# A gated linear-attention and bilinear-GLU kernel on one core: gate/up and q products in another seven-product form, more output rows in seven products, and an order that is computed in the builder

## The chip, the core and the metric

The kernel runs on one core of a Trainium2 chip. The core has a matrix engine (TensorE: PE, with its weight loads shown as PEld), a vector engine (VectorE: DVE), a scalar engine (ScalarE: ACT), a general engine (GpSimd: POOL) and SyncE (SP). In this kernel SP and POOL mostly issue DMAs; those that add to what is already in the destination are issued by POOL. Each engine works through its own list of instructions in the order of the program, and semaphores make it wait for the others.

The metric is the device time of one execution in microseconds (us). Three runs of the kernel before took 590.53, 592.59 and 592.73 us; the median is 592.59.

## What is computed

```python
def _A_ref(x, wqkv, wo):                      # linear attention, 32 heads of 16
    qkv = ...                                 # x @ wqkv, split in q, k, v
    phi = lambda t: jnp.where(t > 0, t + 1, jnp.exp(t)) + 1e-6
    pq, pk = phi(q), phi(k)
    kv = jnp.einsum("bhsd,bhse->bhde", pk, v)
    z = jnp.einsum("bhsd->bhd", pk)
    num = jnp.einsum("bhqd,bhde->bhqe", pq, kv)
    den = jnp.einsum("bhqd,bhd->bhq", pq, z)[..., None] + 1e-6
    return (num / den, heads joined) @ wo

def _B_ref(x, w_gate, w_up, w_down):          # bilinear GLU
    h = (x @ w_gate) * (x @ w_up)
    return h @ w_down

g = _sigmoid((x * gate_w).sum(-1, keepdims=True))
out = g * a + (1 - g) * b
```

x is 2048 x 512 (tokens by features), the hidden width of the GLU is 1792, everything is float32.

## The kernel before, in words

**Numbers in two parts.** A float32 operand is split in a rounded high part (an ACT copy) and a low part (a DVE subtraction), and a product is three matmuls: high by high, high by low, low by high (`mm3`, line 79 for every matmul). So nearly all matmuls have the same shape, 128 x 128 by 128 x 512.

**Phase 1** (16 tiles of 128 tokens) makes k, its feature map and the sums that attention needs (tiles `pk`, `gt`). Beside it x is split for the first pair, and the weights of the first two units are got ready: a dictionary `todo` says after which token tile each step is issued.

**Phase 2** works on transposed data: the tokens in two pairs of blocks of 512 columns, and for each pair 16 *units*. A unit is one 128-wide slice of gate and up (14 of them, kind "f") or one pair of q slices (2 of them, kind "q"). Its 2 x 2 block product (two token blocks by two weights, each sum over two halves of the features) is done in seven products of six matmuls each in place of eight (`unit`, from line 523): sums of x blocks (`xa`, `xb`, `xc1`, `xc4`, `xc6`) and sums of weight blocks (`wr`, split to `wch`, `wcl`) go in, and the products gather in four PSUM banks Y, X, R and S.

**A unit's weights.** `w_load` gets three blocks of 128 x 256, `w_add` makes four more on ACT (two instructions of 512 columns) and adds to five blocks with one POOL DMA of 640 KB, `w_high` and `w_low` split all seven in three parts. There are two raw buffers (`wr`) and two of each split part, so the load for unit n+2 can begin when unit n's weights are split.

**Down projection.** A hidden slice and its rows of w_down (or an attention slice and rows of a product with wo) is one *row*; two rows are a *row pair*. A plain row pair is eight jobs of six matmuls (`down_jobs`, tile `pdn`), each job's result added on DVE to an accumulator `acc`. In the seven-product form (`seven`, banks `sa` and `sb`) a row pair is seven jobs of six matmuls, and several row pairs are chained in one *lot*, so that PSUM is emptied once in a lot; each job needs a split x block (ACT and DVE), and each step a split block of weights (`ws`, `wh`, `wl`), some of them sums made by POOL DMAs. Of the 18 row pairs, 12 are in the seven-product form (four in the first token pair, eight in the second).

**The order.** The units are written out by hand with ten named places in each (`PLACES`). The tables `FIRST` and `SECOND` say how many jobs go to PE between which products; other tables say at which place a step of attention, a load or a split is issued; `advance` lets the chains of the next jobs proceed by leads.

Of the kernel before, what the change touches and what calls it, by code (L numbers as in the profile page):

```python
# [31 lines left out]
LEAD_X = 4  # L32
LEAD_W = 17
GAP_L = 6
GAP_A = 14
HB = 8
FIRST_SEVEN = (((4, 5), (6, 7)), (('a', 0), (8, 9)))
FIRST_AT = (4, 8)
MINUS_AT = (1, 2, 3)
XAT = (11, 6, 4, 8, 11, 7, 11, 13, 13, 13, 10, 13)  # L40
WUNIT = (8, 5, 2)
FIRST = (
    (3, 1, 3, 0), (0, 3, 2, 1), (0, 0, 1, 1), (2, 0, 1, 0), (0, 1, 0, 2), (0, 0, 0, 1), (1, 2, 0, 2), (0, 3, 0, 0),
    (0, 0, 2, 2), (0, 2, 3, 1), (2, 1, 1, 1), (3, 2, 0, 2), (2, 0, 1, 0), (3, 3, 3, 3), (1, 2, 0, 0), (3, 0, 2, 3),
)
PLACES = "high low e m c d t s r end".split()
ATT = ((0, 8, 5, 4, 6, 4, 5, 3), (0, 5, 12, 5, 0, 9, 4, 13))
NS = 58
SECOND = (
    (2, 1, 1, 0), (0, 0, 1, 3), (2, 1, 0, 3), (1, 0, 0, 0), (0, 1, 0, 2), (0, 0, 1, 2), (2, 0, 0, 2), (0, 2, 0, 1),  # L50
    (0, 2, 1, 2), (2, 2, 2, 0), (0, 0, 2, 1), (0, 3, 3, 1), (0, 3, 1, 0), (2, 2, 0, 1), (3, 0, 2, 3), (3, 1, 0, 2),
)
STARTS = (0, 4, 4, 10)
MOST = (2, 2, 2, 2)
MOST_0 = (1, 1, 2, 2)
LEAD_X0 = 4
LEADS_0 = (15, 7, 12)
RELOAD = ((0, 1), (0, 2), (3, 4), (5, 6))
Q_AFTER = ((5, 9), (0, 3))

SLOT = {3: 0, 4: 1, 2: 2, 5: 3, 1: 4, 6: 5, 7: 6}
# [3 lines left out]
def gated_mix(ctx: ExitStack, tc, xt, xp, x, wqkv, wq, wq_add, wo, wgu, wgu_add, wdn, gate_w, out):  # L71
# [39 lines left out]
    def dma_add(dst, src):  # L111
# [17 lines left out]
    own = {i: [const.tile([P, 2, CH], F32R, name=f"xc{i}{v}") for v in "hl"] for i in (1, 4, 6)}  # L129
    xc = {2: [v[:, 0:2] for v in xa], 7: [v[:, 2:4] for v in xa],  # L130
          3: [v[:, 0:2] for v in xb], 5: [v[:, 2:4] for v in xb], **own}


    zeros = own[1][0][:, 0, 0:CH // 2].bitcast(mybir.dt.bfloat16)
# [9 lines left out]
    xsum = {i: dram.tile([P, 2, CH], F32, name=f"xsum{i}") for i in (1, 5, 6, 7)}  # L144
# [28 lines left out]
    def w_add(n):  # L173

        if n < len(order):
            _, kind, m = order[n]
# [12 lines left out]
    def w_low(n, part):  # L189
        if n < len(order):  # L190
# [5 lines left out]
    SUMS = {1: (A1, B2, 0), 3: (B1, B2, 1), 4: (A2, A1, 1), 6: (A1, B1, 0), 7: (A2, B2, 0), 2: (None, A1, 0),  # L196
            5: (None, B2, 0)}

    def x_load(tile_, pair, i, ks):
        dma(tile_, xp[pair, SUMS[i][1]][:, ks])  # L200

    def x_add(tile_, pair, i, ks):
        one, _, sub = SUMS[i]
        if sub:
            act(tile_, tile_, scale=-1.0)
        if one is not None:
            dma_add(tile_, xp[pair, one][:, ks])
# [4 lines left out]
    with tc.tile_pool(name="p1", bufs=2, reuse_waits="tile") as p1:  # L212
# [127 lines left out]
        def cb_load(i):  # L340
            cbs[i] = p1.tile([P, 2, CH], F32, tag="cbs", name="cbs", bufs=3)
            x_load(cbs[i], 0, i, slice(0, 2))

        for t, i in zip((6, 7, 9, 10, 12), (4, 1, 6, 7, 3)):
            plan(t, lambda i=i: cb_load(i))
            plan(t + 2, lambda i=i: x_add(cbs[i], 0, i, slice(0, 2)))
            plan(t + 5, lambda i=i: split(*xc[i], cbs.pop(i)))
        for n, t in ((0, 8), (1, 11)):
            plan(t, lambda n=n: w_load(n))
            plan(t + 2, lambda n=n: w_add(n))  # L350
        plan(14, lambda: w_high(0))
        for part in range(3):
            plan(14 + part // 2, lambda part=part: w_low(0, part))
        plan(16, lambda: w_load(2))
# [36 lines left out]
    p2 = ctx.enter_context(tc.tile_pool(name="p2", bufs=1, reuse_waits="tile"))  # L391
    live = []
    spare, kept = [], {}

    class Buf:

        def __init__(self, name, rounded=False):
            self.home = rounded and bool(spare)
            one = spare.pop(0) if self.home else p2.tile([P, CH], F32R if rounded else F32, tag="s", name=name, bufs=NS)
            self.f = one.bitcast(F32) if rounded else one  # L400
            self.r = one
            if not self.home:
                live.append(self)
                assert len(live) <= NS, clock[0]

    def put(*some):
        for one in some:
            if one.home:
                spare.append(one.r)
            else:  # L410
                live.remove(one)

    def two(name):
        return [Buf(name + v, True) for v in "hl"]

    def split_buf(name, src, copy="act"):

        hi, lo = two(name)
        split(hi.r, lo.r, src, copy)
        return hi, lo  # L420


    at = {}

    def later(n, place, fn):
        at.setdefault((n, place), []).append(fn)

    def do(n, place):
        for fn in at.pop((n, place), []):
            fn()  # L430
        clock[0] += 1
# [13 lines left out]
    def always():  # L445
        return True
# [800 lines left out]
```

## Time and profile before

| what | value |
|---|---|
| median of three runs | 592.59 us |
| the profiled execution, first to last instruction | 591.5 us |
| TensorE clock granted, mean | 0.999 |
| PE busy | 583.7 us (99%) |
| DVE busy | 491.3 us (83%) |
| ACT busy | 364.9 us (62%) |
| POOL busy | 100.3 us (17%) |
| moved by DMA | 106.19 MB |

Busy times are those of the instructions themselves. Matmuls overlap in the pipeline (one is shown as some 390 ns, while the next begins 227 ns later), so PE time is best read from the starts of matmuls: how many begin in a stretch, and where a stretch has fewer. The view by windows gives such counts, the view of waits names who released an engine that stood idle, and the chain that ended last shows the work in order of time.

### The profile page before, as it was taken

What the parts mean: (1) busy time and instruction counts of PE and PEld (TensorE: products, weight loads), DVE (VectorE), ACT (ScalarE), POOL (GpSimd) and SP (SyncE); (2) the same over time, 40 slices, a digit from 0 to 9 for tenths busy, and PEclk for the clock granted to TensorE, in tenths of its full rate; (3) what the DMA queues carried; (4) which work ended last, traced back from release to release, by engine and by line L of the source; (5) the groups of instructions that cost most, each with busy time, mean ns of one, the idle gap of its engine ahead of it and who ended that gap; (6) DMA issues with size and microseconds to landing.
All of it is one profiled execution on the core that took longest, in us unless ns stands there. A gap on an engine that the chain in (4) does not pass through costs nothing.

```text
span 591.5 us, 7915 instructions
## 1 busy us (share of the span) xinstructions
PE 583.7 (99%) x2610; PEld 478.0 (81%) x2610; DVE 491.3 (83%) x798; ACT 364.9 (62%) x649; POOL 100.3 (17%) x123
## 2 busy tenths in 40 slices
PE   9999999999999999999999999999999999999997
PEld 6888888888888868788888788888888888888886
DVE  6877895775567889999869967998798999799987
ACT  3856774677647475688456747458956846646520
POOL 0011100000151124111020042305010322301000
PEclk9999999999999999999999999999999999999999
DMA  9476946868898879556798699779875676834003
GB/s 296 168 201 129 284 106 197 213 194 225 252 225 205 204 211 208 146 120 161 213 239 248 211 221 224 226 155 244 215 168 133 176 148 148 186 71 63 0 2 142
DMA packets 68249, 106.19 MB, mean 180 GB/s; under 512 B 8864, under 2 KB 40352, under 8 KB 68192
## 3 DMA queue, kind: packets, MB, share of 16 engines
q1 hardware_dynamic: 51872, 68.98, 35.5%
q0 software_dynamic: 16048, 36.18, 34.9%
q10 hardware_dynamic: 288, 0.52, 0.3%
q8 instruction: 20, 0.33, 0.2%
q14 instruction: 21, 0.17, 0.1%
HBM read 90.70 MB, written 15.61 MB: 180 GB/s over the span
## 4 chain that ended last, share of the span: by engine, by line
PE 90%; DVE 5%; issue 2%; DMA 2%; ACT 1%; POOL 0%; DVEq 0%; POOLq 0%; ACTq 0%
PE bY L79 13%; PE bX L79 13%; PE bR L79 13%; PE sa L79 11%; PE pdn L79 9%; PE sb L79 8%; PE pk L79 8%; PE gt L79 7%; PE bS L79 7%; DMA wr<-in_wgu_add 2%; DVE wcl L88 1%; DVE acc L88 1%; PE warm L79 1%; PE pw L79 0%; DVE cross L88 0%
## 5 line engine op out<-in xcount | busy, mean ns | idle before, releaser
L88 DVE TENSOR_TENSOR wcl<-wr,wch 128x512 fp32r<-128x512 f32 (+1 forms) x96 | 73.2, 772 | 2.0 <-ACT wch L85 1.9
L85 ACT ACTIVATE wch<-wr 128x512 fp32r<-128x512 f32 (+1 forms) x96 | 60.3, 691 | 4.9 <-DMA wr<-in_wgu_add 4.6
L112 POOL DMA_DIRECT2D wr<-in_wgu_add x28 | 25.0, 892 | 207.7 <-ACT wr L85 153.4
L79 PE MATMUL bX<-xbh,wch 128*128 128x512 f32 x128 | 47.3, 390 | 0.0
L79 PE MATMUL bX<-xbl,wch 128*128 128x512 f32 x128 | 47.2, 389 | 0.0
L79 PE MATMUL bX<-xbh,wcl 128*128 128x512 f32 x112 | 43.6, 389 | 0.0
L85 ACT ACTIVATE cross<-bY 128x512 f32<-128x512 f32 x32 | 19.0, 594 | 33.4 <-PE bY L79 33.3
L88 DVE TENSOR_TENSOR bR<-bX,m 128x512 f32<-128x512 f32 x32 | 22.2, 695 | 20.5 <-PE bX L79 19.6
L85 ACT ACTIVATE m<-bY 128x512 f32<-128x512 f32 x32 | 19.0, 593 | 31.7 <-PE bY L79 31.7
L112 POOL DMA_DIRECT2D ws<-dminus x27 | 31.1, 1341 | 35.7 <-DVE wl L88 24.7
L85 ACT ACTIVATE wr<-wr 128x512 f32<-128x512 f32 x64 | 36.4, 618 | 0.3 <-DMA wr<-in_wgu 0.3
L85 ACT ACTIVATE xh<-cross 128x512 fp32r<-128x512 f32 x38 | 23.5, 626 | 20.7 <-DVE cross L88 19.7
L88 DVE TENSOR_TENSOR t<-bR,cross 128x512 f32<-128x512 f32 x32 | 22.0, 687 | 15.0 <-PE bR L79 6.9
L88 DVE TENSOR_TENSOR acc<-pdn,acc 128x512 f32<-128x512 f32 (+1 forms) x39 | 25.4, 671 | 8.1 <-PE pdn L79 7.9
L85 ACT ACTIVATE cross<-bX 128x512 f32<-128x512 f32 x32 | 19.0, 593 | 21.3 <-DVE bS L88 21.2
L79 PEld LDWEIGHTS bX<-xbh,wch 128*128 128x128 f32 x128 | 24.0, 188 | 5.3 <-ACT cross L85 0.3
L79 PEld LDWEIGHTS bX<-xbl,wch 128*128 128x128 f32 x128 | 24.0, 188 | 5.0
L88 DVE TENSOR_TENSOR xl<-cross,xh 128x512 fp32r<-128x512 f32 x38 | 25.9, 684 | 2.4 <-ACT xh L85 2.2
L79 PE MATMUL bS<-xah,wch 128*128 128x512 f32 x64 | 25.1, 392 | 0.7 <-DVE bS L88 0.7
L112 POOL DMA_DIRECT2D ws<-in_wdn x18 | 24.1, 1721 | 9.1 <-DMA ws<-in_wdn 9.1
L79 PE MATMUL pdn<-hl,dh 128*128 128x512 f32 (+1 forms) x65 | 25.2, 388 | 0.0
L79 PE MATMUL pdn<-hh,dl 128*128 128x512 f32 (+1 forms) x65 | 25.1, 386 | 0.0
(310 smaller groups left out, 1823.6 us busy)
## 6 DMA issues: line engine op xcount, KB each, us to landing
wr<-in_wgu_add POOLq DMA_DIRECT2D x28, 640.0 KB, 6.9
wr<-in_wgu SPq DMA_DIRECT2D x28, 384.0 KB
ws<-in_wdn SPq DMA_DIRECT2D x45, 128.0 KB
xraw<-in_x SPq DMA_DIRECT2D x16, 256.0 KB
terms<-zq SPq DMA_DIRECT2D x16, 256.0 KB
zt<-terms SPq DMA_DIRECT2D x16, 256.0 KB
rb<-den SPq DMA_DIRECT2D x16, 256.0 KB
ws<-dminus POOLq DMA_DIRECT2D x27, 128.0 KB, 4.8
```

Source lines behind the costliest of these rows:

```text
L79: tc.keep_in_program_order(nc.tensor.matmul(*args, **kw))
L85: pin(nc.scalar.activation(dst, src, func, **kw))
L88: pin(nc.vector.tensor_tensor(dst, a, b, op=op))
L112: tc.keep_in_program_order(nc.gpsimd.dma_start(dst, src, accum_op=ALU.add))
```

## The change

Nothing changes in what is computed or in the matmul work of phase 1. Four things are different.

1. **Units: seven products in a form with chained sums.** The products run in the order 1, 5, 6, 2, 7, 3, 4 through banks Y, X, R, Y, R, S, R. Product 1 is copied from Y to R by ACT, product 6 is added to it there, then product 7 and product 4 go on in the same bank; product 5 is copied out once by ACT (`m5`) and added twice by DVE. DVE makes two sums in a unit where it made three; ACT makes three copies in both.
2. **A unit's weights: one chain of sums.** Each new block is the sum before it with one block more, so four blocks are made instead of four copies and five additions in one DMA: ACT copies 256 columns, POOL adds 128 KB, ACT copies 256, POOL adds 128 KB, ACT copies 512, POOL adds 256 KB, each waiting for the one ahead. Blocks 0 to 2 need no sum and are split first. The sums of x are chained in the same way.
3. **Down projection.** 16 of 18 row pairs are in the seven-product form. Lots have one to three row pairs (table `LINE`); the first row pair of the first token pair and the last of the second are plain.
4. **The order.** Phase 2 is written down first as a list of operations with a cost and the buffers that they read and write (`mix`). A model of the engines and DMA rings is then played in the builder (`run`): PE takes from two lines, units and jobs, so that the count of jobs follows the table `SHARE`; each other engine takes the ready operation with the earliest due time. The order in which the model started them is the order of the program. The tables of places are gone.

```diff
-    def w_add(n):
-            act(raws[n][:, 3:5], raws[n][:, 0:1].to_broadcast([P, 2, 2 * P]))
-            act(raws[n][:, 5:7], raws[n][:, 0:2], scale=-1.0)
-            dma_add(raws[n][:, 2:7], (wgu_add if kind == "f" else wq_add)[m])
-    PARTS = ((0, 2), (2, 4), (4, 7))
+                act(raw[:, 3:4], raw[:, 2:3])
+                dma_add(raw[:, 3:4], more[:, 0:1], 0.72)
+                act(raw[:, 4:5], raw[:, 3:4], scale=-1.0)
+                dma_add(raw[:, 4:5], more[:, 1:2], 0.72)
+                act(raw[:, 5:7], raw[:, 4:5].to_broadcast([P, 2, 2 * P]))
+                dma_add(raw[:, 5:7], more[:, 2:4], 1.41)
+    PARTS = ((0, 3), (3, 5), (5, 7))
...
+            product(1, "Y", True)
+            act(bk["R"], bk["Y"])
+            product(5, "X", True)
+            act(m5.f, bk["X"])
+            product(6, "R")
+            tt(bk["S"], bk["R"], m5.f, ALU.add)
+            product(2, "Y")
+            act(cross[0].f, bk["Y"], scale=-1.0 if turned[0] else 1.0)
+            product(7, "R")
...
+                tt(cross[1].f, bk["R"], m5.f, ALU.add)
+            product(3, "S")
+                tt(cross[1].f, bk["S"], cross[1].f, ALU.mult)
+            product(4, "R")
+            tt(cross[0].f, bk["R"], cross[0].f, ALU.mult)
...
-FIRST_SEVEN = (((4, 5), (6, 7)), (('a', 0), (8, 9)))
+LINE = (
+    (0, ((0, 1),)),
+    (0, ((2, 3), (4, 5), (6, 7))),
+    (0, (('a', 0), (8, 9), (10, 11))),
+    (0, ((12, 13), ('a', 1))),
+    (1, ((0, 1), (2, 3))),
+    (1, (('a', 0), (4, 5), (6, 7))),
+    (1, (('a', 1), (8, 9), (10, 11))),
+    (1, ((12, 13),)),
+)
...
+                if engine == "PE":
+                    some = [heads[s][at[s]] for s in "uj" if at[s] < len(heads[s])]
+                    if len(some) == 2 and at["j"] < share(at["u"]):
+                        some.reverse()
+                    for op in some:
+                        if open_[op] and may(op, t):
+                            return take(op, t)
+                    return
+                for op in sorted(ready[engine], key=lambda op: (late[op], op.id)):
+                    if may(op, t):
+                        return take(op, t)
```

Three places show what this does to the lists of the engines. The first is ACT in unit 3 of the first token pair (units count from 0), before: the weights of unit 4 are split in one go (`wch_1475` from the raw blocks `wr_1251`), and the raw blocks of unit 5 (`wr_1385`) get both of their instructions behind them, ahead of unit 3's last bank copy (`cross1_1451<-bX_1396`).

```order
L85 ACTIVATE cross0_1450<-bY_1395 128x512
L85 ACTIVATE half_1303<-half_1303 128x512
L85 ACTIVATE pws_1469<-pw_1465 128x512
L85 ACTIVATE minus_1472<-pws_1469 128x256
L85 ACTIVATE wch_1475<-wr_1251 128x512 x2
L85 ACTIVATE wch_1475<-wr_1251 128x768
L85 ACTIVATE wr_1385<-wr_1385 128x512 x2
L85 ACTIVATE minus_1492<-wdr_1198 128x256
L85 ACTIVATE cross1_1451<-bX_1396 128x512
```

Now the raw blocks of unit 4 are `wr_1252` and their split is `wch_1403`. In unit 2, two of the three instructions on them and the first two parts of the split stand among the bank copies `m5_1328` and `cross0_1365`, with the first ones for unit 5 (`wr_1341`):

```order
L504 ACTIVATE m5_1328<-bX_1308 128x512
L504 ACTIVATE minus_1338<-wdr_1156 128x256
L504 ACTIVATE wr_1252<-wr_1252 128x256
L504 ACTIVATE minus_1343<-pws_1303 128x256
L504 ACTIVATE minus_1346<-wdr_1166 128x256
L504 ACTIVATE cross0_1365<-bY_1291 128x512
L504 ACTIVATE wr_1341<-wr_1341 128x256
L504 ACTIVATE wr_1252<-wr_1252 128x512
L504 ACTIVATE pws_1393<-pw_1322 128x512
L504 ACTIVATE wch_1403<-wr_1252 128x768
L504 ACTIVATE wch_1403<-wr_1252 128x512
L504 ACTIVATE wr_1341<-wr_1341 128x256
```

The last part of unit 4's split stands behind the first bank copy of unit 3 (`bR_1417`):

```order
L504 ACTIVATE bR_1417<-bY_1396 128x512
L504 ACTIVATE wch_1403<-wr_1252 128x512
L504 ACTIVATE minus_1429<-pws_1393 128x256
L504 ACTIVATE m5_1441<-bX_1422 128x512
L504 ACTIVATE wr_1341<-wr_1341 128x512
```

What moved: where one instruction in a unit's turn needed the landing of a POOL DMA (the first of the split), three do now (the second and third `wr<-wr`, and the last of the split), each with bank copies behind it; a unit's split still ends within the unit ahead of it.

The second place is POOL in the same units, before: one addition for each unit, with an x block of the second pair (`cb`) among them.

```order
L112 DMA wr_1251<-in_wgu_add 128x1280
L112 DMA wr_1385<-in_wgu_add 128x1280
L112 DMA wr_1534<-in_wq_add 128x1280
L112 DMA cb_1636<-in_xp 128x512
L112 DMA wr_1671<-in_wgu_add 128x1280
```

Now, three for each unit, and nothing else among them:

```order
L526 DMA wr_1252<-in_wgu_add 128x256 x2
L526 DMA wr_1341<-in_wgu_add 128x256
L526 DMA wr_1252<-in_wgu_add 128x512
L526 DMA wr_1341<-in_wgu_add 128x256
L526 DMA wr_1341<-in_wgu_add 128x512
L526 DMA wr_1433<-in_wq_add 128x256 x2
L526 DMA wr_1433<-in_wq_add 128x512
L526 DMA wr_1520<-in_wgu_add 128x256 x2
L526 DMA wr_1520<-in_wgu_add 128x512
```

What moved: each unit's one addition is three, and the x block stands behind these units now.

The third place is DVE in one unit, before: three sums through the banks (`bR`, `t`, `bS`), with three parts of the next unit's split (`wcl`) among them, and two gate products (`cross1`, `cross0`).

```order
L88 TENSOR_TENSOR bR_1397<-bX_1396,m2_1399 128x512
L88 TENSOR_TENSOR hl_1373<-cross0_1286,hh_1372 128x512
L88 TENSOR_TENSOR dl_1417<-wdr_1198,dh_1416 128x512
L88 TENSOR_TENSOR t_1489<-bR_1397,cross0_1450 128x512
L88 TENSOR_TENSOR wcl_1476<-wr_1251,wch_1475 128x512
L88 TENSOR_TENSOR bS_1398<-t_1489,bX_1396 128x512
L88 TENSOR_TENSOR wcl_1476<-wr_1251,wch_1475 128x512
L88 TENSOR_TENSOR wcl_1476<-wr_1251,wch_1475 128x768
L88 TENSOR_TENSOR cross1_1451<-bR_1397,cross1_1451 128x512
L88 TENSOR_TENSOR cross0_1450<-bS_1398,cross0_1450 128x512
```

Now two sums (`bS` and `cross1`, both with `m5`), the two gate products, and the split in a piece of its own:

```order
L511 TENSOR_TENSOR wcl_1407<-wr_1252,wch_1403 128x768
L511 TENSOR_TENSOR wcl_1407<-wr_1252,wch_1403 128x512 x2
L511 TENSOR_TENSOR bS_1450<-bR_1417,m5_1441 128x512
L511 TENSOR_TENSOR cross1_1476<-bR_1417,m5_1441 128x512
L511 TENSOR_TENSOR cross1_1476<-bS_1450,cross1_1476 128x512
L511 TENSOR_TENSOR cross0_1461<-bR_1417,cross0_1461 128x512
```

What moved: a sum is gone, and the next unit's split (`wcl_1407`) stands in one piece ahead of the sums, not between them.

Counted over the whole lists, PE has 2564 rows where it had 2588 (matmuls, the eight weight loads of the warm-up and two branches; 192 fewer write `pdn`, 168 more write `sa` and `sb`, and the units' number is the same), DVE 767 where it had 784, ACT 730 where it had 653, and the additions to `wr` that POOL issues are 96 where there were 32.

More of the change, by code (lines that the diff above doesn't have):

```diff
@@ L1 @@
+import heapq
 from contextlib import ExitStack
@@ L406, in put @@
[L406 to L431, printed above, removed]
-        most = MOST if n >= units else MOST_0
-        advance(dve=most[0], act=most[1])
@@ L1143, in plain @@
-    def plain(n):
-        return order[n][1] == "f" and (order[n][0], order[n][2]) not in row_of
-    ffn = [n for n in range(len(order)) if plain(n)]
-    def d_load(i):
-        if i < len(ffn):
-            n = ffn[i]
-            wdr[n] = Buf("wdr")
-            dma(wdr[n].f, wdn[order[n][2]])
-    d_load(0)
-    wp_load()
-    g_evac()
-    d_load(1)
-    rows = []
-    for some, place in SEVEN:
-        later(units + place, "end", lambda some=some: jobs.extend(
-            seven(1, [fps[1, key] for key in some], some == SEVEN[-1][0])))
@@ L1198 @@
+        for pair, some in LINE:
+            if len(some) == 1:
+                plain(pair, some[0])
+            else:
+                seven(pair, some)
+        plan(todo_ops, units)
+    mix()
 def kernel(A_x, A_wqkv, A_wo, B_x, B_w_gate, B_w_up, B_w_down, gate_w):
```

1475 lines of the change are left out of this document (791 added, 684 removed).

## The prediction

> **What bounds the kernel now.** I read the page's first part and the chain that ended last, then the windows, then the waits of PE, then the chain in order of time.
>
> ```profile
> span 591.5 us, 7915 instructions
> PE 583.7 (99%) x2610; PEld 478.0 (81%) x2610; DVE 491.3 (83%) x798; ACT 364.9 (62%) x649; POOL 100.3 (17%) x123
> ...
> PE 90%; DVE 5%; issue 2%; DMA 2%; ACT 1%; POOL 0%; DVEq 0%; POOLq 0%; ACTq 0%
> ```
>
> PE is the bound: it is busy nearly all the time, and nine tenths of the chain is matmul work. A busy PE need not be at its peak, so I count how many matmuls (x) begin in equal stretches. The columns are the stretch, its length, the busy times of PE, PEld, DVE, ACT and POOL, the granted clock, the DMA share and GB/s.
>
> ```profile
> 200.00:250.00 50.00, 48.69 (x211) 38.71 (x209) 44.95 (x72) 28.78 (x52) 12.37 (x14) 1.00 0.81 193
> 250.00:300.00 50.00, 49.30 (x215) 39.97 (x215) 46.58 (x77) 36.76 (x67) 5.22 (x6) 1.00 0.69 165
> 300.00:350.00 50.00, 49.31 (x217) 40.14 (x216) 40.75 (x62) 31.05 (x52) 7.13 (x9) 1.00 0.85 240
> 350.00:400.00 50.00, 50.00 (x222) 41.28 (x221) 44.65 (x72) 27.35 (x49) 15.05 (x20) 1.00 0.82 199
> 400.00:450.00 50.00, 50.00 (x222) 41.39 (x221) 44.24 (x73) 40.06 (x74) 11.45 (x13) 1.00 0.80 195
> ...
> 550.00:570.00 20.00, 20.00 (x90) 16.57 (x89) 19.65 (x32) 9.44 (x17) 0.00 (x0) 1.00 0.00 1
> ```
>
> A stretch of 50 us without a stall holds 222 matmuls, and the clock is full throughout. Three stretches hold 211, 215 and 217, so 11 + 7 + 5 = 23 matmuls are missing. The last row says something else: with DVE busy for 19.65 of 20 us PE still lost nothing. A full DVE is not in itself a stall.
>
> ```profile
> PE sb L79 <- ACT xh L85: 1.1, 1, 1.1
> PE sa L79 <- ACT xh L85: 0.7, 1, 0.7
> PE bS L79 <- DVE bS L88: 0.7, 1, 0.7
> PE sb L79 <- DVE xl L88: 0.2, 1, 0.2
> ...
> 1.26 3.61 PE warm L79 x8
> ...
> 348.23 5.44 PE pdn L79 x24
> ...
> 576.80 11.02 PE pdn L79 x54
> ```
>
> The waits say who was late: three times a split x block for a job of a seven-product lot (`sa`, `sb`), once a DVE sum within a unit (`bS`). The last rows are pieces of the chain (start, length). They give the pitch, 5.44 / 24 = 0.227 us a matmul, so the 23 missing ones are **5.2 us** of stalls. They also give the ends: 1.3 us before the first matmul, and 591.5 - 576.80 - 11.02 = 3.7 us behind the last piece. Both ends do the same work after the change.
>
> **The change, part by part.** *Matmuls removed.* Four more row pairs go from eight jobs to seven, six matmuls each: 24 fewer, as the lists say (2588 to 2564). The row of 24 matmuls above prices them without any conversion: **-5.4 us**. They stand on the bound, so all of it is gained unless PE waits more. Units keep their 42 matmuls, phase 1 its own.
>
> *Stalls removed.* The order that caused the 5.2 us no longer exists. I take all of them out and put the new order's in by three terms. None of the three can be below nothing, since the old stalls are already out.
>
> ```profile
> L85 ACT ACTIVATE cross<-bY 128x512 f32<-128x512 f32 x32 | 19.0, 594 | 33.4 <-PE bY L79 33.3
> L85 ACT ACTIVATE wch<-wr 128x768 fp32r<-128x768 f32 x32 | 26.6, 833 | 0.0
> L85 ACT ACTIVATE wch<-wr 128x512 fp32r<-128x512 f32 x64 | 36.8, 620 | 4.9 <-DMA wr<-in_wgu_add 4.6 <-DMA wr<-in_wq_add 0.3
> L88 DVE TENSOR_TENSOR bR<-bX,m 128x512 f32<-128x512 f32 x32 | 22.2, 695 | 20.5 <-PE bX L79 19.6 <-ACT m L85 0.6
> L88 DVE TENSOR_TENSOR wcl<-wr,wch 128x768 fp32r<-128x768 f32 x32 | 30.4, 949 | 0.0
> ```
>
> *(i) Hand-overs within a unit.* Product 6 adds to what ACT copied from Y to R, and only product 5 lies between: 6 x 0.227 = 1.36 us of cover. The copy is like `cross<-bY`, 0.594 us. If ACT has just begun a wide split (0.833), the two take 1.43 us, so a bad case costs 0.1 us and some hand-over, 0.3 at most as I estimate it. The sum into S (0.695, behind a `wcl` of 0.949) is alike. Bounds: 0 to 32 x 0.3 = 10 us. The nearest row is the old form's own hand-over of this kind, which cost (`bS`) a wait of 0.7 us in 32 units. I take 1.
>
> *(ii) The chain of weight sums.*
>
> ```profile
> wr<-in_wgu_add POOLq DMA_DIRECT2D x28, 640.0 KB, 6.9
> ...
> ws<-dminus POOLq DMA_DIRECT2D x27, 128.0 KB, 4.8
> ...
> cb<-in_xp POOLq DMA_DIRECT2D x10, 256.0 KB, 6.4
> ...
> ws<-in_wdn POOLq DMA_DIRECT2D x18, 128.0 KB, 6.6
> ...
> 60.52 0.43 SPq L109 DMA_DIRECT2D wr<-in_wgu  x1
> ...
> 67.25 1.15 ACT L85 ACTIVATE wr<-wr 128x512 f32<-128x512 f32 x2 [0.32 <-DMA wr<-in_wgu]
> ```
>
> The last number of a DMA row is its median time from issue to landing. One addition of 6.9 us becomes three, one behind the other: 4.8 + 4.8 + 6.4 = 16.0 us. The load took up to 67.25 - 60.52 = 6.7 us. With three ACT instructions (at most 0.62 each) and the last split (0.62 + 0.68) a raw buffer is held for some 6.7 + 1.9 + 16.0 + 1.3 = 25.9 us. There are two buffers, so PE keeps its pace where two units last longer. An early unit with one job beside it is 48 matmuls, 10.9 us, and two are 21.8 us: short by 4.1 us. But in those units POOL issues nothing else (the lists in the section on the change), while the medians come from crowded stretches.
>
> ```profile
> DMA to landing us min/median/max: 5.8/6.9/9.8
> DMA to landing us min/median/max: 2.9/6.0/11.8
> DMA to landing us min/median/max: 3.8/6.4/11.2
> ```
>
> These are the answers for the tiles `wr`, `ws` and `cb`. At the minima the chain is 2.9 + 2.9 + 3.8 = 9.6 us and the buffer is held for 19.5 us, less than 21.8; later units have some four jobs each (112 and 16 plain ones for 32 units) and last 15 us. The lists also end a unit's split within the unit ahead, so a late chain has most of a unit to give before PE waits for weights. What can hurt at once is ACT itself: it stands in the wait for a landing with a bank copy behind it. Bounds: 0, and 4.1 / 2 x 8 early units = 16 us. I take 1.5, near the lower end, because of the empty queue and of that slack.
>
> The Trainium skill, page "DMA: Bandwidth & Descriptors", sections "Anatomy of one DMA — SWDGE (gpsimd) path" and "Rules for kernel authors", speaks against this edit: each DMA has a fixed cost of about 2.0 us beside bytes / 436e3, and many small transfers should be made one. By its figures, one of 640 KB is an estimated 3.5 us and the three are 7.2 us, so the chain would grow by 3.7 us and still fit, and this term would be 0. The trace's 640 KB took 5.8 us at best, so the rows disagree with the size and I keep to them; that splitting costs is common to both.
>
> *(iii) Jobs of the seven-product form.* Most of the old stalls were theirs: 2.0 of the 2.7 us of waits above, so by that share 3.9 of the 5.2 us, in 12 x 7 = 84 jobs. There are 16 x 7 = 112 now. Bounds: 0, and at the old rate 3.9 x 112 / 84 = 5.2 us.
>
> ```profile
> L88 DVE TENSOR_TENSOR acc<-pdn,acc 128x512 f32<-128x512 f32 x37 | 24.7, 684 | 8.0 <-PE pdn L79 7.9
> L88 DVE TENSOR_TENSOR t<-bR,cross 128x512 f32<-128x512 f32 x32 | 22.0, 687 | 15.0 <-PE bR L79 6.9
> ```
>
> DVE loses one sum in each unit (32 x 0.687 = 22 us) and 32 additions of plain jobs (32 x 0.684 = 22 us), and what the extra jobs bring makes it 17 instructions fewer in all, 12 us of 491. ACT gains 77; at 0.6 each at most that is 46 us on 365, some 70% of the span. Neither becomes the bound on average, but jobs stand closer together in places. I take 2, below the middle.
>
> **The sum.** 591.5 - 5.4 - 5.2 + (1 + 1.5 + 2) = 585.4 us for the profiled span. The median of the runs is 592.59 - 591.5 = 1.1 us above it, so I predict **586.5 us**.
>
> **Rivals.** *The stalls all but vanish.* Without the three terms the time is 586.5 - 4.5 = 582.0. For it: most of the hold-ups have cover; against it: a list of in-order engines with 83% on DVE seldom has none.
>
> *The saving is given back by DVE where jobs crowd.* By the rows, a lot of two row pairs (14 jobs, 19 us of PE) takes about 14 `xl`, 7 `wl`, 8 sums and 10 bank additions, 39 x 0.685 = 27 us of DVE; a unit takes three `wcl` (2.3 us) and four others (2.8), 5.1 us in 9.5 of PE. DVE is full once jobs are over half of PE's time. The average is a third, but in the last units jobs outnumber products. If it is over by 5 to 10% through some 60 us, PE loses 3 to 6 us more: 590 to 593. Against it stands the row of 550 to 570 us, full without a loss.
>
> *Slower: ACT held by the additions.* Three waits on landings stand among each unit's bank copies. The cover of the copy into R leaves about 0.5 us once the copy (0.594) and hand-overs are taken from 1.36. If landings come 1.9 us later than the order assumed (4.8 against 2.9), each such copy pays 1.4 us. At 16 of 32 units that is 22 us in place of the 1.5: 607. It is slower than before by over 0.5% from 8 units on. Against it: in the old trace ACT lost only 4.9 us in all to `wr` landings, and the first of the three waits has nothing urgent close behind it.
>
> *The change doesn't remove what it says.* The lists show the 24 rows gone; I give this nothing.
>
> **How the numbers follow.** Two runs differ by some 2 us, and 0.5%, 3 us, is about what a measurement can tell from no change: faster is below 589.6, slower above 595.6. My forecast with stalls between 1.5 and 7.5 us (583.5 to 589.6) has a chance of 0.52, the vanished stalls 0.18, the saving given back 0.20, and ACT held 0.10. So faster has 0.70, the same 0.20, slower 0.10. The range is 582.5 to 594.5: it leaves out some 0.06 below, where not even the hand-overs cost anything, and 0.12 above, the slower rival with the upper edge of the one before it.
>
> **What would show it.** In the new profile, a 50 us stretch without a stall must still hold 222 matmuls, and the last piece end about 4 us before the span; then the first term is right. The matmuls missing from the stretches times 0.227 are the new stalls, 4.5 us if I am right. PE waiting for `bR` copied by ACT speaks for (i); ACT waiting for `wr<-in_wgu_add` by more than some 10 us for the slower rival; PE waiting for `xh`, `xl`, `wh` or `wl` while DVE is full for the crowded jobs. I am wrong if matmuls come at another pitch, or if a stall comes from a place that I did not price: phase 1's x sums, or the change of token pair.

## The result, and the profile after

| | before | after |
|---|---|---|
| median of four runs each | 591.56 us | 615.28 us |
| lowest to highest | 590.50 to 592.73 | 613.29 to 619.93 |
| ratio, 95% interval | | 1.0416 (1.0371 to 1.0461) |

The kernel is 4.2% slower, 28.8 us above the forecast and outside its range. The profiled execution is the slowest of the four (619.93 us). The first part of its page, with the chain's shares by engine and by line:

```profile
span 618.2 us, 8117 instructions
PE 587.5 (95%) x2586; PEld 473.2 (77%) x2586; DVE 470.1 (76%) x781; ACT 385.2 (62%) x726; POOL 152.2 (25%) x180
...
PE 44%; DMA 23%; issue 14%; ACT 8%; DVE 6%; POOL 4%; SPq 1%; POOLq 0%; DVEq 0%; ACTq 0%
```

24 matmuls are gone, as foreseen. But matmuls, 90% of the chain before, are 44% now, and DMA has gone from 2% to 23%. The windows (columns as before: PE, PEld, DVE, ACT, POOL, clock, DMA share, GB/s):

```profile
200.00:250.00 50.00, 49.52 (x214) 39.59 (x213) 38.47 (x65) 34.83 (x69) 15.81 (x19) 1.00 0.71 146
250.00:300.00 50.00, 47.75 (x205) 37.91 (x204) 43.73 (x75) 35.15 (x69) 16.76 (x20) 1.00 0.91 223
300.00:350.00 50.00, 44.59 (x189) 36.12 (x188) 39.68 (x65) 34.48 (x64) 13.89 (x16) 0.97 0.91 238
350.00:400.00 50.00, 47.39 (x206) 38.23 (x205) 44.99 (x72) 36.92 (x71) 17.50 (x20) 1.00 0.78 173
400.00:450.00 50.00, 45.90 (x195) 36.66 (x194) 39.57 (x64) 35.95 (x69) 13.11 (x15) 0.98 0.71 163
```

Against 222 in a stretch without a stall, these five lack 8, 17, 33, 16 and 27 matmuls: 101 x 0.227 = 23 us. The stretches before and behind them have smaller gaps. No engine other than PE is full (DVE at most 45 of 50 us). The loss is in waits, and in many places. The waits of PE, then ACT, then SyncE's queue (total, times, longest):

```profile
PE bR L533 <- ACT bR L504: 10.0, 7, 2.8
PE bR L533 <- DVE cross L511: 8.9, 6, 3.6
PE bR L533 <- DVE bS L511: 3.2, 2, 2.2
...
ACT wr L504 <- DMA wr<-in_wgu_add: 48.2, 27, 4.5
ACT wch L504 <- DMA wr<-in_wgu_add: 10.4, 8, 4.2
...
SPq L522 <- DMA wr<-in_wgu_add: 71.8, 13, 12.4
```

PE waits for products' banks (`bR`), which ACT and DVE hand over, and ACT waits for the landings of the units' weight sums: 48.2 us in the chain's copies, where it was 4.9 us for all such landings before. The landings themselves, by the list of DMA issues (number, size, median us):

```profile
wr<-in_wgu_add POOLq DMA_DIRECT2D x56, 128.0 KB, 4.2
wr<-in_wgu_add POOLq DMA_DIRECT2D x28, 256.0 KB, 4.6
ws<-dminus POOLq DMA_DIRECT2D x36, 128.0 KB, 5.0
```

How one becomes the other is seen in the chain in order of time (start, length) at the longest stall:

```profile
304.13 5.91 DMA wr<-in_wgu_add
310.07 0.43 ACT wr L504
310.50 0.28 issue
310.78 7.46 DMA wr<-in_wgu_add
318.26 0.63 ACT wr L504
318.89 0.52 ACT wch L504
319.41 0.31 ACT wr L504
319.72 0.53 ACT xh L504
...
324.30 0.61 DVE cross L511
324.95 2.93 PE bR L533 x6
```

The first addition lands 5.9 us after its issue, ACT copies at once, the second takes 7.5 us, and ACT copies again; only then come the split that a job needs (`xh`), DVE's part and the bank sum `cross` for which product 4 (`bR`) waits. DVE stood still too: its next instruction, `wcl` of the weights being made, waited 4.58 us for ACT's `wch` and began at 319.44 us, with `xl` and `cross` behind it. Those weights belong to a later unit (PE was at the last product of its own), so nothing of them was urgent; what stood behind them in the lists of ACT and DVE was.

### The profile page after: what moved, and what is told of

It reads as the page before. It is cut to its first block, busy times and chain, and to the rows that moved or that the text cites. A ratio compares the mean times of both kernels' runs of the same rounds, so it can differ in the third digit from the quotient of the medians.

```text
span 618.2 us, 8117 instructions
## 1 busy us (share of the span) xinstructions
PE 587.5 (95%) x2586; PEld 473.2 (77%) x2586; DVE 470.1 (76%) x781; ACT 385.2 (62%) x726; POOL 152.2 (25%) x180
## 3 DMA queue, kind: packets, MB, share of 16 engines
q0 software_dynamic: 24768, 29.37, 31.2%
## 4 chain that ended last, share of the span: by engine, by line
PE 44%; DMA 23%; issue 14%; ACT 8%; DVE 6%; POOL 4%; SPq 1%; POOLq 0%; DVEq 0%; ACTq 0%
DMA wr<-in_wgu_add 11%; PE bR L533 10%; PE sa L533 7%; PE sb L533 6%; PE bY L533 6%; PE pk L73 4%; PE gt L73 3%; DMA ws<-dminus 3%; PE bS L533 3%; PE bX L533 3%; PE pdn L533 2%; POOL wr L526 2%; DMA ws<-in_wdn 2%; ACT wch L504 2%; DMA cb<-in_xp 1%
## 5 line engine op out<-in xcount | busy, mean ns | idle before, releaser
L526 POOL DMA_DIRECT2D wr<-in_wgu_add x78 | 76.1, 997 | 230.3 <-ACT wr L504 203.1
L504 ACT ACTIVATE wr<-wr 128x256 f32<-128x256 f32 (+1 forms) x90 | 43.1, 486 | 70.6 <-DMA wr<-in_wgu_add 48.2
L504 ACT ACTIVATE wch<-wr 128x512 fp32r<-128x512 f32 (+1 forms) x93 | 61.7, 696 | 23.8 <-DMA wr<-in_wgu_add 10.4
L533 PE MATMUL bR<-xc6h,wch 128*128 128x512 f32 x64 | 27.0, 421 | 10.2 <-ACT bR L504 10.0
L533 PE MATMUL bR<-xbh,wch 128*128 128x512 f32 x64 | 26.3, 412 | 8.9 <-DVE cross L511 8.9
L533 PE MATMUL bY<-xal,wch 128*128 128x512 f32 x80 | 31.1, 389 | 0.0
L511 DVE TENSOR_TENSOR bS<-bR,m 128x512 f32<-128x512 f32 x32 | 22.2, 692 | 10.2 <-ACT m L504 3.6
L533 PE MATMUL bR<-xc7h,wch 128*128 128x512 f32 x64 | 25.8, 404 | 3.4 <-DVE bS L511 3.2
L533 PEld LDWEIGHTS bR<-xc6h,wch 128*128 128x128 f32 x64 | 12.2, 191 | 18.0 <-ACT bR L504 15.7
L533 PE MATMUL bR<-xc6l,wch 128*128 128x512 f32 x64 | 25.5, 399 | 0.0
L533 PE MATMUL bR<-xc6h,wcl 128*128 128x512 f32 x64 | 25.5, 399 | 0.0
L533 PE MATMUL bR<-xbl,wch 128*128 128x512 f32 x64 | 25.4, 398 | 0.0
L533 PE MATMUL bR<-xbh,wcl 128*128 128x512 f32 x64 | 25.4, 397 | 0.0
```

Of the source, the lines that this page charges most:

```text
L504: return Op("ACT", lambda: pin(nc.scalar.activation(get(dst), get(src), func, **{k: get(v) for k, v in kw.items()})), c, c + 0.11, [src, * ...
L511: return Op("DVE", lambda: pin(getattr(nc.vector, name)(get(dst), *[get(v) for v in ins], **kw)), c, c + 0.085, some, [dst], kind="dve")
L526: return Op("POOL", lambda: pin(nc.gpsimd.dma_start(get(dst), get(src), accum_op=ALU.add)), 0.54, 0.0, [src, dst], [dst], work=work, kind= ...
L533: tc.keep_in_program_order(nc.tensor.matmul(get(dst), get(lhs), get(rhs), **kw))
```

## The experiments

The first theory, **A**: the order leaves the chained additions no margin, ACT stands in order in the waits for their landings, and the bank copies behind it are late. Rivals: **B**, the hand-overs of the new bank form are too tight by themselves; **C**, the denser seven-product jobs and the weight sums of their lots.

### Which part of the change it is

`e1_no_unit_sums`: the units' additions emit nothing, their place in the order stays.

```diff
-                dma_add(raw[:, 3:4], more[:, 0:1], 0.72)
+                dma_add(raw[:, 3:4], more[:, 0:1], 0.72).fn = lambda: None
...
```

> The kernel after (615.3 us) with the 84 chained additions of the units' weight sums left out (the three per unit that GpSimd starts, for units 2 to 31; the slots keep what ACT copied there), every other instruction in the same order. Theory A (ACT stands in order in waits for the landings of these additions, with the units' bank copies behind it): most of the excess over the 585.4 us that the matmuls need goes, 585 to 593 us, and the row of ACT waiting for wr from in_wgu_add (48.2 us) is gone without another taking its place. Rival B (the copy of Y into R and the two hand-overs behind it are too tight by themselves) and rival C (the denser seven-product jobs and their weight sums): 607 to 616 us.

587.29 us, ratio to before 0.9925 (0.9899 to 0.9951): 28 us come back. Its windows at the worst places of after, and its largest wait of PE for a bank:

```profile
300.00:350.00 50.00, 50.00 (x221) 41.36 (x222) 49.42 (x80) 43.34 (x81) 8.80 (x10) 1.00 0.77 219
...
400.00:450.00 50.00, 50.00 (x221) 41.25 (x221) 40.24 (x67) 36.38 (x69) 2.63 (x3) 1.00 0.49 137
...
PE bR L533 <- ACT bR L504: 1.2, 2, 1.0
```

221 matmuls each, where there were 189 and 195. Bank form, jobs and order are the same, and the wait for the copy into R falls from 10.0 to 1.2 us, so B and C by themselves cannot be most of it.

`e2_no_lot_sums`: the same with the lots' `ws` additions.

```diff
-                                dma_add(half(five, i), block(i, *of), 0.72)
+                                dma_add(half(five, i), block(i, *of), 0.72).fn = lambda: None
...
```

> The kernel after with the additions of the output lots' weight sums left out (the ws additions that GpSimd starts, 128 KB each), every other instruction in the same order. Theory A: these share the queue with the units' additions and a few splits wait for them, so a part comes back, 605 to 613 us. Rival C: 585 to 595 us. Rival B: 613 to 617 us.

600.85 us, 1.0163 (1.0114 to 1.0212). More than I expected for A, less than for C: 14 us. ACT's wait for `wr` from `in_wgu_add` is still 36.0 us. The two kinds of additions share one queue and delay each other: without the units' additions those of the lots (`ws<-dminus`) land after 4.0 us in place of 5.0, and without the lots' the first two of a unit land after 3.8 in place of 4.2 (the third not sooner: 4.9 for 4.6). So what taking each away brings (28 and 14 us) can't be added up to one loss.

`e4_no_copy_into_r`: no copy of Y into R.

```diff
-            act(bk["R"], bk["Y"])
+            act(bk["R"], bk["Y"]).fn = lambda: None
...
-            product(6, "R")
+            product(6, "R", True)
```

> The kernel after without ACT's copy of Y into R in each of the 32 units (product 6 starts the bank, so product 1 is left out of the sums in R and S); everything else in the same order. Rival B: below 600 us, the waits of PE for bR copied by ACT (10.0 us) gone with what follows from them. Theory A: ACT still stands in the waits for landings, with the other bank copies behind it; PE's 10 us of waits for that copy go in part, and 0.6 us of ACT a unit: 604 to 612 us.

613.72 us, 1.0347 (1.0286 to 1.0408), which overlaps the interval of after and lies above what either theory gave. The copy into R is not the cause: without it PE waits for `bS` (8.0 us, where it was 3.2) and `cross` (9.4). The other hand-overs of the bank form are not taken out here; that they cost little without the additions is shown by e1 alone.

### Waits or bytes

Does it cost that instructions wait for the landings, or that the additions exist beside other transfers? `e8_sums_elsewhere` adds to scratch memory that nothing reads:

```diff
+    spare = dram.tile([P, 4, 2 * P], F32, name="spare")
...
+        dma(spare, wgu_add[0])
...
+                dma_add(raw[:, 3:4], more[:, 0:1], 0.72).fn = lambda: pin(
+                    nc.gpsimd.dma_start(spare[:, 0:1], more[:, 0:1], accum_op=ALU.add))
```

> The kernel after with the 84 chained additions of units 2 to 31 still issued by GpSimd from the same addresses and in the same sizes, but added to a scratch array in DRAM that nothing reads, so that no instruction waits for their landing (and the weight sums are not formed). The order on the other engines is the same. Theory A in its strict form (the wait for the landing is what costs): 586 to 593 us, as without the additions (587.3). Rival D (the additions' traffic, or GpSimd's work for them, slows the other transfers and engines): 600 to 615 us.

602.60 us, 1.0196 (1.0157 to 1.0234). This is in the range of rival D and far from that of the strict theory A: with no wait for these sums left, 15.3 us over e1 remain. But GpSimd waits there for its own earlier landings (84 us in all), which after does not have. `e13_sums_aside` has four scratch arrays in turn (`spare[n % 4]`) and no load into them:

> As e8_sums_elsewhere, but the additions go to four scratch arrays in turn, so that GpSimd does not wait for its own earlier landings (55 to 90 us of such waits there), and nothing else is loaded. Theory A, strict (only the waits for the landings cost): 586 to 592 us. Rival D (the additions' traffic and GpSimd's time for issuing them delay the other loads and the lots' additions): stays at 597 to 605 us; then ACT and the splits wait for wr from in_wgu and for ws.

610.31 us, 1.0304 (1.0276 to 1.0333), above both ranges, but PE stands still once for 10.4 us: the additions, held by nothing, run ahead at the start of phase 2, and PE waits for the loads of `wv` there. Without that stall it would be an estimated 600 us (610.3 - 10.4), near e8. `e14_sums_out` mends that by taking the data from the slot that ACT has just copied:

```diff
+                dma_add(raw[:, 3:4], more[:, 0:1], 0.72).fn = lambda: pin(
+                    nc.gpsimd.dma_start(spare[n % 4][:, 0:1], get(raw[:, 3:4]), accum_op=ALU.add))
```

> As e13_sums_aside, but the additions take their data from the raw slot that ACT has just copied (to the scratch arrays in DRAM), so that GpSimd issues each of them at the same point as in the kernel after and not ahead of its time, which cost e13 one stall of 10.4 us on the loads of wv. Nothing waits for their landing but the reuse of the slot two units later. If the waits for the landings are most of the loss: 589 to 597 us. If the additions' traffic and issue are most of it: 602 to 612 us.

601.68 us, 1.0179 (1.0135 to 1.0223): between the two ranges. By this run ACT's waits for the sums are some 13.6 us (615.3 - 601.7) and the rest, 14.4 us over e1, comes without them. It is an estimate: the additions go to DRAM here, and landed after 4.8 and 5.4 us in place of 4.2 and 4.6. Its waits of PE, of ACT for the loads, and of SyncE's queue, then SyncE's in `e16_margin`, a run that comes below:

```profile
PE bR L534 <- ACT bR L505: 4.3, 3, 3.7
PE bR L534 <- DVE cross L512: 3.2, 4, 2.0
...
ACT wr L505 <- DMA wr<-in_wgu: 24.0, 12, 5.2
...
SPq L523 <- DMA spare<-wr: 87.3, 18, 11.8
```

```profile
SPq L522 <- DMA wr<-in_wgu_add: 73.8, 15, 11.0
```

SyncE, in order too, stands before the next load into the slot; that is one candidate for the rest. The runs speak against it as the main part: e8 has no such wait and is no faster than e14, and e16 has as much of it as after (73.8 us and 71.8) and takes 18.8 us less. The other candidate is the transfers themselves: ACT waits 24.0 us for the loads (`wr<-in_wgu`) in e14 and 24.4 in e8, where e1 has 11.4. `e18_eighth` keeps every addition and wait and cuts the bytes:

```diff
+                    nc.gpsimd.dma_start(get(raw[:, 3:4])[:, :, 0:32], more[:, 0:1, 0:32], accum_op=ALU.add))
```

> The kernel after with each of the 84 chained additions cut to the first 32 of the 256 columns of its blocks (an eighth of the bytes; the sums are formed in these columns alone): as many additions, descriptors, issues and waits for landings as before the cut, in the same order. If the waits for the landings cost by the fixed part of a landing: 606 to 614 us (landings of 128 KB were 4.2 us in the median; 3 us or more is left). If the bytes cost, in these landings and in the loads and lots' additions beside them: 590 to 602 us.

595.74 us, 1.0047 (1.0024 to 1.0071): seven tenths of the 28 us follow the bytes, though all the waits are kept. The number of packets doesn't: GpSimd's queue has 28608 here and 24768 in after. Its landings:

```profile
wr<-in_wgu_add POOLq DMA_DIRECT2D x52, 16.0 KB, 3.3
wr<-in_wgu_add POOLq DMA_DIRECT2D x26, 32.0 KB, 3.3
ws<-dminus POOLq DMA_DIRECT2D x36, 128.0 KB, 4.3
```

So fewer bytes make each landing about 1 us shorter, 0.7 us for the lots' additions, and ACT's wait for the chain falls from 48.2 to 29.4 us. Whether the shorter landings or the room for the other transfers brought more isn't separated here. `e15_one_addition` has the bytes and one landing:

```diff
-                dma_add(raw[:, 3:4], more[:, 0:1], 0.72)
...
-                dma_add(raw[:, 4:5], more[:, 1:2], 0.72)
...
-                dma_add(raw[:, 5:7], more[:, 2:4], 1.41)
+                dma_add(raw[:, 3:7], more, 2.8)
```

> The kernel after with one addition of 512 KB onto all four slots in place of the chain of three (128, 128 and 256 KB): the same copies on ACT, the same bytes, one landing to wait for, and no copy between landings; the sums are not the ones needed. The order is worked out anew with the model's old numbers. If the chain's repeated waits are what costs: 588 to 597 us. If the bytes cost: 603 us or more.

600.51 us, 1.0149 (1.0122 to 1.0175), between its two ranges. The chain is part of it, not all. Yet the kernel before moved more bytes through this queue with no more than 5.2 us of stalls. The DMA queue that GpSimd feeds, of before and then of after (packets, MB, share of 16 engines):

```profile
q0 software_dynamic: 16048, 36.18, 34.9%
```

```profile
q0 software_dynamic: 24768, 29.37, 31.2%
```

What differs, beside the number of additions and packets, is the order. So theory A is kept in a wider form, to be put to the test: it is the missing margin for landings, on every queue that waits for one.

### Margin in the order

The model in the builder lets an addition of 128 KB land after 1.42 + 0.72 + 1.42 = 3.56 us at the least and one of 256 KB after 4.25, later only while other transfers of the model are under way; ACT's copy may start at that instant if ACT is free, with no margin. The trace has 4.2 and 4.6 in the median and up to 9.6. `e5_later_a` gives 0.76 us more:

```diff
-        IN, OUT, PART = {"SP": 1.07, "POOL": 1.42}, {"SP": 0.82, "POOL": 1.42}, {"SP": 1.0, "POOL": 2.0}
+        IN, OUT, PART = {"SP": 1.07, "POOL": 1.8}, {"SP": 0.82, "POOL": 1.8}, {"SP": 1.0, "POOL": 2.0}
```

> The kernel after, with the order worked out anew from a model in which a DMA that GpSimd starts lands 0.76 us later (its two fixed parts of 1.42 us set to 1.8 us). Nothing else is changed. Theory A: ACT meets fewer landings that are still under way, the ACT waits for wr from in_wgu_add fall by half or more, and the time falls to 592 to 606 us. Rivals B and C: the landings don't matter, 611 to 618 us.

608.65 us, 1.0288 (1.0261 to 1.0315), less than A gave and more than the rivals; ACT's wait fell to 34.3 us, by less than half. `e10_issue_1us_later` sets the cost of an issue on GpSimd to 1.0 (it was 0.54) as well:

> The kernel after with the order worked out from a model in which GpSimd is busy 1.0 us for each DMA that it starts (0.54 in the model of the kernel after, 0.997 in its trace) and a landing comes 0.76 us later. Theory A: closer to the chip than the later landing alone (608.7 us), 594 to 604 us. If only the landing's own time counts: 606 to 611 us.

601.19 us, 1.0179 (1.0151 to 1.0207). My reason was wrong, though: issues in the trace after start down to 0.535 us apart, so 0.54 was right and the records of 0.997 overlap; the larger cost acts as more margin. `e16_margin` keeps that cost and adds 1.76 us to a landing (`"POOL": 1.6` in IN, `3.0` in OUT):

> The kernel after with the order worked out from a model in which an addition by GpSimd lands 1.76 us later than in the kernel after (0.76 in e10_issue_1us_later, 601.2 us). If lack of margin is what remains there: 592 to 598 us. If margin is used up: 600 to 606 us.

596.50 us, 1.0071 (1.0044 to 1.0098). The program has the operations of after, 18.8 us sooner, with nothing changed but numbers in a model. ACT's wait for these landings is 12.7 us in place of 48.2:

```profile
ACT wr L504 <- DMA wr<-in_wgu_add: 12.7, 11, 3.8
```

Each of these three models gives a new order to every engine, not to these copies alone. An order that is new but has no more margin was not run; for margin speak the four times that fall in step with it (615.3, 608.7, 601.2, 596.5) and the wait that falls with them.

### Other ways to form the sums

`e9_pool_sums` loads the four blocks into the slots and sums them on GpSimd; `e12_pool_sums_later` does so with e10's numbers.

```diff
+                dma(raw[:, 3:7], more, 1.52)
+                for dst, a, b, op in ((3, 3, 2, ALU.add), (4, 4, 3, ALU.subtract), (5, 5, 4, ALU.add), (6, 6, 4, ALU.add)):
...
+                    Op("POOL", lambda dst=dst, a=a, b=b, op=op: pin(nc.gpsimd.tensor_tensor(get(dst), get(a), get(b), op=op)),
```

> The kernel after with the sums of units 2 to 31 formed in place by GpSimd: the four blocks to be added are loaded straight into the slots by one more load, and four tensor_tensor of 128x256 on GpSimd replace three copies on ACT and three additions by DMA. The order is worked out anew (cost 1.0 us for one such sum in the model). Theory A: ACT no longer stands in a wait for a landed sum, so the time is near that without additions, 584 to 592 us, below before (591.8) if a sum of GpSimd takes 1.0 us or less. If GpSimd is much slower than that (over 2 us a sum), or slows DVE: 595 to 610 us.

> The sums on GpSimd (as e9_pool_sums) and the model's corrected numbers (as e10_issue_1us_later) together. Theory A: the lots' additions, worth 14 us in e2_no_lot_sums, get room in the order too: 581 to 588 us, below before and below e9_pool_sums by 1 to 5 us. If the corrected numbers only spread the same waits: equal to e9_pool_sums within 2 us.

608.37 us, 1.0289 (1.0252 to 1.0326), and 608.44 us, 1.0286 (1.0251 to 1.0321). Both are what was set down for a GpSimd that slows DVE, or for waits that only spread. ACT waits for no landed sum any more, but GpSimd now waits for the loads. The groups of e9, with `wcl` of after last, show one reason why it isn't faster (count, then busy us and mean ns):

```profile
L940 POOL TENSOR_TENSOR wr<-wr 128x256 f32<-128x256 f32 x120 | 138.7, 1184 | 220.6 <-DMA wr<-in_wgu_add 54.2 <-DMA wr<-in_wgu 52.9 <-DVE cross L511 36.9
...
L511 DVE TENSOR_TENSOR wcl<-wr,wch 128x512 fp32r<-128x512 f32 x62 | 49.7, 819 | 2.9 <-ACT wch L504 2.8
...
L511 DVE TENSOR_TENSOR cross<-bR,cross 128x512 f32<-128x512 f32 x28 | 19.2, 685 | 5.9 <-PE bR L533 5.0 <-ACT hh L504 0.7
```

```profile
L511 DVE TENSOR_TENSOR wcl<-wr,wch 128x512 fp32r<-128x512 f32 x62 | 41.8, 683 | 16.5 <-ACT wch L504 16.3
```

Beside GpSimd's sums, DVE's `wcl`, with both operands in SBUF, takes 819 ns in place of 683; `cross`, with one operand in PSUM, stays at 685. In all, DVE is busy for 504.9 us where after has 470.1, with as many instructions. That can't be the whole reason: `h3_all_on_dve` below has 506.1 us of DVE and is 14 us faster. The rest is not shown.

Three kernels with e10's numbers move the sums to DVE. The first sum is then added onto its own loaded block, without a copy. `h1_last_on_dve` forms the last two by one DVE sum, `h2_two_on_dve` the last three blocks on DVE, `h3_all_on_dve` all. The edit of h1:

```diff
-                act(raw[:, 3:4], raw[:, 2:3])
-                dma_add(raw[:, 3:4], more[:, 0:1], 0.72)
+                dma_add(raw[:, 3:4], more[:, 2:3], 0.72)
...
-                act(raw[:, 5:7], raw[:, 4:5].to_broadcast([P, 2, 2 * P]))
-                dma_add(raw[:, 5:7], more[:, 2:4], 1.41)
+                tt(raw[:, 5:7], raw[:, 1:3], raw[:, 4:5].to_broadcast([P, 2, 2 * P]), ALU.add)
...
-    FIRST, ADD = "11 12 22", "21 11 22 12"
+    FIRST, ADD = "11 22 12 21", "21 11 22 12"
```

> The first sum of a unit is added onto its block loaded in place (no copy by ACT), the last two are formed by one VectorE sum of 128x512; one copy on ACT and two additions of 128 KB by DMA are left of three and three. The model has the corrected numbers of e10_issue_1us_later (601.2 us). Theory A: two of three waits on ACT go, 588 to 596 us. If DVE (20 us more) is now too full: 598 us or more.

> Only the first sum of a unit is an addition by DMA; the other two sums are formed on VectorE (31 us more for DVE, 43 us less for ACT). Theory A: ACT waits for no landing of these but in the splits, 584 to 592 us. If DVE is too full: 595 us or more.

> All three sums of a unit on VectorE (some 42 us more for DVE, to 512 us), no addition by DMA for units 2 to 31. Theory A: no wait on a landing is left but that of the load, 583 to 590 us, below before (591.5) by 0.3 to 1.4%. If DVE, full to 87%, becomes the bound in the crowded stretches: 592 to 600 us, with PE waiting for bS, cross or xl.

595.81 us, 1.0066 (1.0048 to 1.0085); 595.87 us, 1.0064 (1.0041 to 1.0088); 594.10 us, 1.0041 (1.0026 to 1.0057). All three are far better than after and none reaches before. h1 came out as A gave it; h2 and h3 lie in the ranges for a DVE that is too full (495 and 506 us). `e17_margin_and_dve` is h1 with e16's margin and 0.68 us more for SyncE's loads:

```diff
-        IN, OUT, PART = {"SP": 1.07, "POOL": 1.8}, {"SP": 0.82, "POOL": 1.8}, {"SP": 1.0, "POOL": 2.0}
+        IN, OUT, PART = {"SP": 1.07, "POOL": 1.6}, {"SP": 1.5, "POOL": 3.0}, {"SP": 1.0, "POOL": 2.0}
```

> h1_last_on_dve (595.8 us) with 1.76 us of margin for the additions and 0.68 us for SyncE's loads. If what is left there are late landings of loads and first sums: 587 to 592 us, level with or below before (591.6). If it is DVE that is full: 594 to 598 us.

**585.57 us, 0.9892 (0.9862 to 0.9922): 1.1% below before, and 29.7 us below after.** Its span and engines, two windows, and the waits that answer to those of after:

```profile
span 585.4 us, 8011 instructions
PE 577.1 (99%) x2586; PEld 474.4 (81%) x2586; DVE 486.0 (83%) x811; ACT 363.1 (62%) x666; POOL 126.0 (22%) x150
...
350.00:400.00 50.00, 50.00 (x222) 41.41 (x221) 50.00 (x83) 33.21 (x60) 14.23 (x17) 1.00 0.71 164
400.00:450.00 50.00, 50.00 (x223) 41.34 (x222) 43.05 (x71) 34.61 (x65) 10.46 (x12) 1.00 0.73 183
...
ACT wr L504 <- DMA wr<-in_wgu_add: 6.4, 5, 3.8
PE bR L533 <- DVE cross L511: 1.8, 3, 1.1
PE bR L533 <- ACT bR L504: 0.5, 1, 0.5
```

222 and 223 matmuls, one of the two stretches with DVE busy for all of its 50 us, so a full DVE was not what held h1 back. More margin is worth 4.7 us with the sums by DMA (e10 to e16) and 10.2 us with the last on DVE (h1 to e17, where SyncE's loads got margin as well).

## Why the prediction was wrong, point by point

- **Matmuls removed, -5.4 us.** Right: 2610 to 2586, and e1 and e17 have them at the same pitch (221 to 223 in 50 us).
- **Old stalls out, -5.2 us.** Right as bookkeeping; the old order is gone.
- **(i) Hand-overs in a unit, +1, and (iii) seven-product jobs, +2.** Nearly right. Without the chain the forecast would have been 585.0 us (586.5 - 1.5); e1 took 587.3, so the two are at most about 5.3 us and not 3, if all that is left over is theirs. PE's waits for `bR` in e1 are 1.7 us in 32 units, so the 0.3 us allowed for one hand-over, which no row shows, was ample. The waits for the copy into R that after shows (10.0 us) are the chain's: with the copy and without the additions e1 has 1.2 us of them.
- **(ii) The chain of weight sums, +1.5.** This step failed. It measured 28.0 us (615.28 - 587.29, the additions alone), above its own upper bound of 16. The bound asked when PE would lack *weights*, by the time that a raw buffer is held, and the choice of the lower end rested on the empty queue and on the slack of the splits. PE never waited for a unit's weights (`wch`, `wcl`) in the waits of after. The slack was real, and the order did not use it: the model lets each of ACT's copies go as soon as the landing that it assumes, among bank copies that are urgent. I named that hold ("What can hurt at once is ACT itself") and gave it no term in the sum.
- **The landings.** I took the minima, 2.9 and 3.8 us, because the queue was empty in early units. For those units it was near the truth: the nine additions of 128 KB issued between 120 and 170 us in after landed after 3.2 us in the median. But the nine between 250 and 350 us, where the DMA share is 0.91, took 5.3, and over the whole span the medians are 4.2 and 4.6.
- **The fourth rival, ACT held by the additions.** It was the right mechanism for about half, if e14 is taken for the measure: its sign (over 10 us of ACT waiting for `wr<-in_wgu_add`) came with 48.2 us. That its 607 comes nearest to 615.3 is in part luck, since it priced nothing of the other half. It also took the order to assume landings of 2.9 us; the model has 3.56. I gave it 0.10 because ACT had lost only 4.9 us to such landings before. But that was a property of the old order. From the starts in the trace, ACT's first instruction that needed an addition (the second of the split, not the first: that reads blocks 0 and 1, which have no sum) came 12.2 us after its issue (median of 32, the shortest 7.7), with a landing of 6.9. In after, the copy behind the second link comes after 4.4 us, with a landing of 4.2; in e16 after 6.4.
- **What I had not seen:** 14.4 us remain when nothing reads the sums (e14). The likely way is that the additions slow the lots' sums and the next loads, for which ACT then waits (24 us for the loads, 11.4 in e1), and that these are placed without margin too. This is argued and not shown: no run gives the loads alone more margin. SyncE's queue, held before the reuse of a slot, can't be most of it, since e8 does without that hold and is no faster.

So the expected gain of 6.1 us was not absent: 4.5 us are there in e1, which leaves the additions out, and 5.9 us in e17, which forms the last sums on DVE. After lost it, and over 20 us more, in an order computed from landing times (3.56 and 4.25 us at the least) that the chip met in 25 of 64 additions of 128 KB and in 11 of 32 of 256 KB.

## What to carry to other kernels

An order computed from a model must be given the landing times of a crowded queue, not the best ones, wherever an in-order engine waits for a landing with urgent work behind it: 1.8 us more for a landing and 0.5 us more for an issue, in the model alone, were worth 18.8 us here. When a step gets a chain of transfers, ask for each wait what stands behind it in the list of the engine that waits, whether or not the transfer's own result is urgent. And price a new order by its slack, since waits that the old profile does not show were hidden by the old order.

## What was unexpected of the hardware

- **GpSimd beside DVE.** A GpSimd sum of two 128x256 blocks takes 1.18 us, and makes DVE sums with both operands in SBUF up to 1.35 times as long (`t`: 921 ns where after has 682; `wcl`: 819 where after has 683), while those with an operand in PSUM keep theirs (`cross<-bR,cross`: 685 and 686). The Trainium skill, page "SBUF — State Buffer", section "Who interferes with whom", says that a DVE operation with two SBUF inputs contends with a GpSimd operation that reads SBUF, since its second input comes through the read interface that the two share, and that one with at most one SBUF input, outside its two-port modes, does not. The trace agrees on both: 819 for 683 with two, 685 with one.
- **The clock after a stall.** In after, two matmuls start 4.0 us apart at 321 us and 3.2 us apart at 445 us; the starts behind these (the first left out) are 427 ns apart in place of 227, six and five times, and the windows there have a granted clock of 0.97 and 0.98. Where two start 2.6 us apart (484 and 538 us), the next interval but one is 236 ns or less. So in these two places a long stall cost at least 1 us more than its own length (five and six times 0.2 us).
- **The fixed part of a landing.** An addition with an eighth of the bytes (16 KB for 128 KB) still lands after 3.3 us where 128 KB took 4.2, both in the median.
